# Another order of the same instructions on all five engines of a one-core kernel

## The chip, the core and the metric

The kernel runs on one core of a Trainium2 chip. A core has five engines, each with its own stream of instructions: TensorE (PE in the profile; its weight loads are listed apart as PEld), VectorE (DVE), ScalarE (ACT), GpSimd (POOL) and SyncE (SP, which here only issues DMAs). They wait for one another through semaphores. On-chip memory is SBUF (128 partitions) and PSUM (8 banks of 128 x 512 f32, written by TensorE). The metric is the device time of one execution in microseconds; lower is better.

## What is computed

Two branches of the same input are mixed by a gate. x has 2048 rows of 512, H = 32 heads of 16, Dff = 1376; everything is bf16.

```python
def _A_ref(x, wqkv, w_phi, wo):
    q, k, v = ...                       # x @ wqkv, split into 32 heads of 16
    pq = jnp.einsum("bhsd,hdf->bhsf", q, w_phi)
    pk = jnp.einsum("bhsd,hdf->bhsf", k, w_phi)
    phi_q = concatenate([softmax(pq), softmax(-pq)], axis=-1)
    phi_k = concatenate([softmax(pk), softmax(-pk)], axis=-1)
    kv = jnp.einsum("bhsf,bhsd->bhfd", phi_k, v)
    z  = jnp.einsum("bhsf->bhf", phi_k)
    num = jnp.einsum("bhqf,bhfd->bhqd", phi_q, kv)
    den = jnp.einsum("bhqf,bhf->bhq", phi_q, z)[..., None] + 1e-6
    return (num / den) ... @ wo
def _B_ref(x, w1, w2):
    return relu(x @ w1) @ w2
g = sigmoid((x * gate_w).sum(-1, keepdims=True))
return g * a + (1 - g) * b
```

## The kernel before

The work is written as a graph of 616 named tasks (`_Graph`, line 81). A task is one or a few instructions of one engine, with the tasks that it depends on. Which task follows which on an engine is a list of names for each engine, `ORDER` (line 17). `schedule` checks that each list holds every task once and that no task stands ahead of one that it needs on its own engine; `emit` then issues the instructions in the order of the list, with a semaphore wait in front of a task wherever a task of another engine, or a DMA, has to be done first. An engine does its list strictly in order, so a task that waits holds up all that stand behind it. (`dur` and `lat` of a task are notes that nothing in the kernel reads.)

The names, with m a tile of 128 rows (16 of them), c a chunk of 512 rows (4), k a block of 128 columns of Dff, and J one of 18 jobs (k0 to k8 and q0 to q8; the first seven of each kind take two tiles, the last two one):

- Head: xa0, xa1 load the first chunk of x; xt and xe transpose it through TensorE (L325) and copy it into XT. wkT, wqT, x1, x2, x3 are transposing loads from HBM (L269). f1_j and f0_j (L356) fold w_phi into the key and query weights, fe1 and fe0 (L317, L319) copy the result. v (L374) makes the values, ve (L379) evicts them.
- Branch B: h (L397) is a block of x @ w1, rl (L415) its relu into HT; hr, rr (L405, L421) do the last 96 columns together with the gate's dot product, which gv (L391) puts into w1 as a column; gr (L423) takes the gate out, and ge, gp, go make its two factors. ht (L426) is a DMA transpose of the last block into HT.
- Feature maps, a chain for each job J: pr (TensorE, L454, bank 0 and 1) -> ev (ScalarE, L479) -> mx and mn (VectorE, L483, L485) -> t1 and t2 (GpSimd, L492) -> ex (ScalarE, L497) -> sm and rc (VectorE, L499, L503, L523) -> for a key job nm (GpSimd, L506), for a query job ra and nm (GpSimd, L525, L529).
- Keys: kv (TensorE, L513) adds a tile to kv and z in banks 6 and 7; after kv15, kn and kz (VectorE, L544, L546) take them out.
- Queries: tq (SyncE, L532) is a DMA transpose of a normalised tile, 256 KB, into one of six places of PHQ; nd (TensorE, L556) two halves of num and den; rd and o (VectorE, L562, L564) divide and apply the gate; to (SyncE, L569) is a DMA transpose of the result, into one of four places of OT.
- Output: b (TensorE, L577; L598 for the last tile) is relu(..) @ w2 for a tile, a (L583, L609) adds the attention branch @ wo in the same bank; oe (ScalarE, L628; L616 and L619 for the last tile) scales and evicts; st (ScalarE's queue, L631) stores 128 KB.

PSUM banks are few: h, b and a share banks 3, 4 and 5 in turn. The bank of a block is set by its number in the graph, not by its place in ORDER, so h0_0, h0_3 and h0_6 share bank 3, and a block waits for the eviction (rl, fe, gr, oe) of the block that had the bank before it. In the same way b2 waits for gr3, b7 for oe4 and b8 for oe5. nd has three banks in turn; ev has three places in PB, ex four in FT.

The order is fixed by hand for the first 19 TensorE tasks, warm0 to h0_0, and for the first tasks of ScalarE, VectorE and GpSimd (`follow`, line 100); the DMA loads keep theirs among themselves.

Of the kernel before, what the change touches and what calls it, by code (L numbers as in the profile page):

```python
# [15 lines left out]

ORDER = {
    "sp": (
        "xa0 wva xa1 wvb w1a wphi wkT w1b x1 gw w1c wqT x2 x3 w2a w2b ht1 wo ht0 tq1 tq0 tq2 tq3 to0 to1 ht2 to2 "
        "tq4 tq5 to3 tq6 tq7 to4 to5 ht3 tq8 tq9 to6 to7 tq11 tq10 to8 to9 tq12 tq13 to11 to10 tq14 tq15 to12 "  # L20
        "to13 to14 to15 st15_1 "
    ),
    "pool": (
# [5 lines left out]
    ),  # L29
    "act": (  # L30
# [8 lines left out]
    ),  # L39
    "dve": (  # L40
# [10 lines left out]
    ),  # L51
# [10 lines left out]
    ),  # L62
}

# [615 lines left out]
```

## Time and profile before

| | us |
|---|---|
| median of the 3 runs shown (lowest, highest) | 151.71 (151.42, 151.9) |
| the profiled execution | 151.17 |
| its span, first to last instruction | 149.2 |
| TensorE: busy, share of the span | 144.9, 97% |
| VectorE | 110.8, 74% |
| GpSimd | 109.7, 74% |
| ScalarE | 91.1, 61% |
| granted TensorE clock | 1.00 of full speed |

The profile covers one execution. It lists each engine's busy time; a group "L454 PE MATMUL PS<-WP,XT" is line 454, TensorE, a matmul that reads the tiles WP and XT and writes PS. Times of matmuls overlap one another in the records, and a few per cent of matmul records can be missing, so the weight loads (PEld) show the order and the holes better than the matmuls do. The wait of an engine is given with what ended it ("<- POOL FT L506"). The DMA view gives for each kind of transfer the count and the median time from issue to landing. The profile names no tasks; a row is put to its task by counting the engine's instructions along its ORDER list, since every engine keeps to its list.

### The profile page before, as it was taken

What the parts mean: (1) busy time and instruction counts of PE and PEld (TensorE: products, weight loads), DVE (VectorE), ACT (ScalarE), POOL (GpSimd) and SP (SyncE); (2) the same over time, 40 slices, a digit from 0 to 9 for tenths busy, and PEclk for the clock granted to TensorE, in tenths of its full rate; (3) what the DMA queues carried; (4) which work ended last, traced back from release to release, by engine and by line L of the source; (5) the groups of instructions that cost most, each with busy time, mean ns of one, the idle gap of its engine ahead of it and who ended that gap; (6) DMA issues with size and microseconds to landing.
All of it is one profiled execution on the core that took longest, in us unless ns stands there. A gap on an engine that the chain in (4) does not pass through costs nothing.

```text
span 149.2 us, 2538 instructions
## 1 busy us (share of the span) xinstructions
PE 144.9 (97%) x968; PEld 73.0 (49%) x984; DVE 110.8 (74%) x169; ACT 91.1 (61%) x127; POOL 109.7 (74%) x73
## 2 busy tenths in 40 slices
PE   7899999999999999999999999999999999999994
PEld 2454444454454645444547445444545454544553
DVE  0542679999995499989569899999979987817501
ACT  3347769997886888966896854476535443303131
POOL 4000599999999999999999999999958795060000
PEclk9999999999999999999999999999999999999999
DMA  5999999500003400000000061847495964787423
GB/s 140 295 199 223 259 166 276 191 0 0 4 2 94 116 7 0 0 0 0 4 0 0 0 141 32 151 104 186 102 172 109 245 156 107 135 208 211 106 73 108
DMA packets 45524, 16.11 MB, mean 108 GB/s; under 512 B 39272, under 2 KB 45256, under 8 KB 45512
## 3 DMA queue, kind: packets, MB, share of 16 engines
q1 hardware_dynamic: 43208, 13.89, 42.3%
q10 hardware_dynamic: 2304, 2.06, 4.3%
q8 instruction: 8, 0.13, 0.4%
q14 instruction: 4, 0.03, 0.1%
HBM read 4.41 MB, written 2.10 MB: 44 GB/s over the span
## 4 chain that ended last, share of the span: by engine, by line
PE 94%; DMA 3%; issue 1%; SPq 1%; DVE 0%
PE PS L577 24%; PE PS L397 23%; PE PS L454 19%; PE PS L374 9%; PE PS L583 9%; PE PS L513 3%; DMA FT<-in_A_x_dram 3%; PE PS L556 3%; PE PS L405 2%; PE PS L598 2%; PE PS L356 1%; PE PS L609 1%; SPq L265 1%; PE PS L325 0%; DVE OSB L619 0%
## 5 line engine op out<-in xcount | busy, mean ns | idle before, releaser
L492 POOL TENSOR_TENSOR TS<-PB,MX 128x1024 bf16<-128x1024 bf16 (+1 forms) x18 | 30.8, 1716 | 13.9 <-DVE MX L483 13.9
L499 DVE TENSOR_REDUCE ZB<-FT 128x128 f32<-128x2048 bf16 (+1 forms) x18 | 36.6, 2037 | 4.6 <-ACT FT L497 4.5
L397 PE MATMUL PS<-XT,W 128*128 128x512 bf16 x155 | 37.7, 379 | 0.3
L577 PE MATMUL PS<-W,HT 128*128 128x512 bf16 (+1 forms) x161 | 37.0, 379 | 0.2
L497 ACT ACTIVATE FT<-TS 128x2048 bf16<-128x2048 bf16 (+1 forms) x18 | 31.0, 1720 | 4.5 <-PE PS L513 2.4
L492 POOL TENSOR_TENSOR TS<-MN,PB 128x1024 bf16<-128x1024 bf16 (+1 forms) x18 | 30.8, 1720 | 0.1
L454 PE MATMUL PS<-WP,XT 128*128 128x512 bf16 x126 | 30.1, 379 | 0.1
L506 POOL TENSOR_TENSOR FT<-FT,SC 128x2048 bf16<-128x2048 bf16 (+1 forms) x9 | 29.5, 3285 | 0.0
L415 ACT ACTIVATE HT<-PS 128x512 bf16<-128x512 f32 x40 | 22.8, 601 | 6.3 <-PE PS L397 6.2
L628 ACT ACTIVATE OSB<-PS,OMG 128x512 bf16<-128x512 f32 x15 | 10.2, 685 | 23.5 <-PE PS L583 23.5
L479 ACT ACTIVATE PB<-PS 128x1024 bf16<-128x1024 f32 (+1 forms) x18 | 16.8, 932 | 12.3 <-PE PS L454 8.1
L577 PEld LDWEIGHTS PS<-W,HT 128*128 128x128 bf16 (+1 forms) x165 | 15.5, 97 | 17.4 <-ACT OSB L628 0.3
L397 PEld LDWEIGHTS PS<-XT,W 128*128 128x128 bf16 x160 | 15.0, 98 | 17.5 <-ACT HT L415 1.0
L483 DVE TENSOR_REDUCE MX<-PB 128x64 bf16<-128x1024 bf16 (+1 forms) x18 | 19.5, 1082 | 5.4 <-ACT PB L479 5.4
L485 DVE TENSOR_REDUCE MN<-PB 128x64 bf16<-128x1024 bf16 (+1 forms) x18 | 19.2, 1075 | 0.3 <-ACT PB L479 0.2
L454 PEld LDWEIGHTS PS<-WP,XT 128*128 128x128 bf16 x128 | 12.1, 98 | 14.0 <-DVE WP L319 0.4
L529 POOL TENSOR_TENSOR FT<-FT,SR 128x1024 bf16<-128x1024 bf16 (+1 forms) x9 | 15.6, 1736 | 0.6
L374 PE MATMUL PS<-WV,XT 128*128 128x512 bf16 x61 | 15.5, 379 | 0.2
L583 PE MATMUL PS<-WO,OT 128*128 128x512 bf16 x58 | 14.4, 378 | 0.1
L564 DVE SCALAR_TENSOR_TENSOR OTM<-PS,EG,RD 128x256 bf16<-128x256 f32 x32 | 14.1, 466 | 0.4
L562 DVE RECIPROCAL RD<-PS 128x16 f32<-128x16 f32 x32 | 7.0, 238 | 8.2 <-PE PS L556 7.9
L379 ACT ACTIVATE VS<-PS 128x512 bf16<-128x512 f32 x16 | 9.5, 607 | 3.0 <-PE PS L374 3.0
(54 smaller groups left out, 96.3 us busy)
## 6 DMA issues: line engine op xcount, KB each, us to landing
out_dram<-OSB ACTq DMA_DIRECT2D x15, 128.0 KB, 2.5
W<-in_B_w_dram SPq DMA_DIRECT2D x1, 1280.0 KB, 8.2
W<-in_B_w_dram SPq DMA_DIRECT2D x2, 512.0 KB, 5.0
FT<-in_A_x_dram SPq DMA_DIRECT2D x2, 256.0 KB, 3.4
WV<-in_A_wqkv_dram SPq DMA_DIRECT2D x2, 256.0 KB, 3.7
WO<-in_A_wo_dram SPq DMA_DIRECT2D x1, 512.0 KB, 4.6
W<-in_B_w_dram SPq DMA_DIRECT2D x1, 352.0 KB, 3.6
PHQ<-FT SPq DMA_TRANSPOSE x16, 2.8
```

Source lines behind the costliest of these rows:

```text
L374: last = q.matmul(PS[:, b, :], XT[:, j, m * P:(m + 1) * P], WV[:, j, :], start=(j == 0), stop=(j == ND - 1))
L397: last = q.matmul(PS[:, b, :], W1[:, j, k * P:(k + 1) * P], XT[:, j, chunk(c)], start=(j == 0), stop=(j == ND - 1))
L415: add(f"rl{a}_{k}", "act", lambda q, a=a, k=k, b=b: q.activation(HT[:, k, chunk(a)], PS[:, b, :], ACT.Relu), (f"h{a}_{k}",), dur=0.6)
L454: last = q.matmul(PS[:, n, :], XT[:, j, m * P:(m + 1) * P], WP[:, s, j, :], start=(j == 0), stop=(j == ND - 1))
L483: add(f"mx_{J}", "dve", lambda q, sl=sl, w=w, i=pbg: q.tensor_reduce(MX[:, sl, 0:w * H], i, AX.X, ALU.max), (f"ev_{J}", old("t1")), dur=0. ...
L485: add(f"mn_{J}", "dve", lambda q, sl=sl, w=w, i=pbg: q.tensor_reduce(MN[:, sl, 0:w * H], i, AX.X, ALU.min), (f"ev_{J}", old("t2")), dur=0. ...
L492: add(f"{tn}_{J}", "pool", lambda q, o3=o3, a3=a3, b3=b3: q.tensor_tensor(o3, a3, b3, ALU.subtract), (f"{'mx' if sg == 0 else 'mn'}_{J}", ...
L497: add(f"ex_{J}", "act", lambda q, fs=fs, ts=ts, w=w: q.activation(FT[:, fs, 0:w * F], TS[:, ts, 0:w * F], ACT.Exp), (f"t1_{J}", f"t2_{J}", ...
L499: add(f"sm_{J}", "dve", lambda q, fs=fs, sl=sl, w=w: q.tensor_reduce(ZB[:, sl, 0:2 * w * H], FT[:, fs, 0:w * F].rearrange("p (g d) -> p g ...
L506: add(f"nm_{J}", "pool", lambda q, f3=f3, sl=sl, w=w: q.tensor_tensor(f3, f3, SC[:, sl, 0:2 * w * H].unsqueeze(2).to_broadcast([P, 2 * w * ...
L577: last = q.matmul(PS[:, ab, :], HT[0:r, k, m * P:(m + 1) * P], W2[0:r, k, :], start=(k == 0), stop=False)
L583: last = q.matmul(PS[:, ab, :], OT[:, m % NOT, t, :], WO[:, t, :], start=False, stop=(t == ND - 1))
```

## The change

The five lists of `ORDER` are replaced by others. No other line differs. Each list holds the same tasks; no instruction, size, buffer, bank or dependency is changed.

```diff
--- before.py
+++ after.py
@@ -16,49 +16,49 @@
 
 ORDER = {
     "sp": (
-        "xa0 wva xa1 wvb w1a wphi wkT w1b x1 gw w1c wqT x2 x3 w2a w2b ht1 wo ht0 tq1 tq0 tq2 tq3 to0 to1 ht2 to2 "
-        "tq4 tq5 to3 tq6 tq7 to4 to5 ht3 tq8 tq9 to6 to7 tq11 tq10 to8 to9 tq12 tq13 to11 to10 tq14 tq15 to12 "
+        "xa0 wva xa1 wvb w1a wphi wkT w1b x1 gw w1c wqT x2 x3 w2a w2b ht1 ht0 tq0 ht2 wo tq1 tq2 tq3 to0 to1 to2 "
+        "tq4 tq5 to3 ht3 tq6 to4 tq7 tq9 tq8 to5 to6 to7 tq10 to8 tq11 tq12 to9 tq13 to10 tq14 tq15 to11 to12 "
         "to13 to14 to15 st15_1 "
     ),
     "pool": (
-        "iota_r iota_i iota_c gwz pads ones t1_k0 t2_k0 t1_k1 t2_k1 t1_k2 t2_k2 nm_k0 t1_k3 t2_k3 t2_k4 t1_k5 "
-        "t1_k4 nm_k2 nm_k1 t2_k5 t2_k6 t1_k6 nm_k3 t1_k8 t1_k7 t2_k7 t2_k8 nm_k4 t2_q0 t1_q0 nm_k5 t1_q1 t2_q1 "
-        "nm_k6 t1_q2 ra_q0 t2_q2 nm_q0 nm_k7 nm_k8 ra_q1 nm_q1 t1_q3 t2_q3 t1_q4 ra_q2 nm_q2 t2_q4 t2_q5 ra_q3 "
-        "nm_q3 t1_q5 t1_q6 ra_q4 nm_q4 t2_q6 ra_q5 nm_q5 t1_q8 t2_q7 t1_q7 t2_q8 ra_q6 nm_q6 ra_q7 nm_q7 ra_q8 "
+        "iota_r iota_i iota_c gwz pads ones t1_k0 t2_k0 t1_k1 t2_k1 t2_k2 t1_k2 nm_k0 t2_k3 t1_k3 t1_k4 t2_k4 "
+        "nm_k1 t1_k5 t2_k6 t1_k6 t2_k5 nm_k2 t2_k7 nm_k3 t1_k7 t2_k8 nm_k4 t1_k8 t1_q0 t2_q0 nm_k5 nm_k6 t1_q1 "
+        "t2_q1 ra_q0 t1_q2 nm_q0 t2_q2 nm_k7 nm_k8 ra_q1 nm_q1 t1_q3 t2_q3 t1_q4 ra_q2 nm_q2 t2_q4 ra_q3 nm_q3 "
+        "t1_q5 t2_q5 ra_q4 nm_q4 t2_q6 t1_q6 t1_q7 t2_q7 ra_q5 nm_q5 ra_q6 nm_q6 t2_q8 t1_q8 ra_q7 ra_q8 nm_q7 "
         "nm_q8 "
     ),
     "act": (
-        "xe00 xe10 xe20 xe30 ve1 ve2 ve3 fe1_1 fe1_3 ve0 rl0_0 ev_k0 rl0_3 rl0_1 rl0_2 ev_k1 rl0_6 rl0_4 ev_k2 "
-        "ex_k0 rl0_5 ev_k3 rl0_9 ex_k1 rl0_8 ev_k4 ex_k2 rl1_0 rl0_7 rl1_1 ev_k5 rr0 ve4 ex_k3 ev_k6 rl1_4 rl1_2 "
-        "ve5 rl1_7 rl1_3 ve6 ev_k7 rl1_5 ve7 rr1 rl1_8 ve8 rl1_6 ve9 rl1_9 ge1 ex_k4 ve10 ev_k8 ex_k5 ve11 rl2_1 "
-        "rl2_2 ev_q0 ex_k6 rl2_4 rl2_0 ev_q1 rl2_5 ve12 ge0 ex_k7 rl2_3 ev_q2 gp0 rl2_6 rl2_9 rl2_7 rl2_8 ve13 "
-        "ev_q3 rl3_1 ex_k8 rl3_0 ex_q0 ve14 rl3_3 ev_q4 rl3_4 gp1 rl3_7 rl3_6 rr2 ex_q1 rr3 ge2 ve15 rl3_2 rl3_9 "
-        "ev_q5 rl3_5 ex_q2 rl3_8 ge3 ev_q6 ex_q3 oe0 oe1 ex_q4 st1 ev_q7 oe2 oe3 ex_q5 st3 ev_q8 oe4 oe5 gp2 "
-        "ex_q6 st2 st4 st0 gp3 oe6 ex_q7 oe7 ex_q8 st7 oe8 oe9 st9 st8 oe10 oe11 st5 st6 st10 st11 oe12 oe14 "
-        "oe13 st12 st13 st14 oe15_0 st15_0 "
+        "xe00 xe10 xe20 xe30 ve1 rl0_0 fe1_3 fe1_1 ve3 ve2 rl0_3 ev_k0 rl0_6 rl0_1 ev_k1 rl0_4 rl0_2 ve0 ev_k2 "
+        "ex_k0 rl0_7 rl0_5 ev_k3 ex_k1 rl0_8 ev_k4 ex_k2 rl0_9 rl1_0 ev_k5 ve4 rr0 rl1_1 ve5 ex_k3 rl1_3 ve6 "
+        "ev_k6 rl1_2 ex_k4 rl1_4 ve7 rl1_7 rl1_6 ve8 rr1 rl1_5 rl1_9 ev_k7 ve9 rl1_8 rl2_0 ev_k8 ex_k5 ve10 "
+        "rl2_3 ev_q0 ex_k6 ve11 rl2_2 ev_q1 rl2_6 rl2_1 ve12 rl2_5 rl2_8 ex_k7 rl2_9 rl2_4 ev_q2 ve13 rl2_7 "
+        "rl3_1 ex_k8 ge1 ev_q3 rl3_0 rl3_4 ex_q0 ve14 gp1 rr2 rl3_3 rl3_7 ev_q4 ex_q1 ve15 rr3 rl3_6 ge3 rl3_2 "
+        "ev_q5 gp3 ge2 rl3_5 ge0 rl3_9 ex_q2 rl3_8 gp0 ev_q6 ex_q3 oe0 gp2 oe1 ex_q4 st0 ev_q7 oe2 oe3 ex_q5 oe4 "
+        "st3 ex_q6 ex_q7 oe5 ev_q8 oe6 oe7 ex_q8 oe8 st4 st1 st6 st2 oe9 st9 oe10 st5 oe11 st10 st7 st11 oe12 "
+        "oe13 oe14 st13 st8 st14 st12 oe15_0 st15_0 "
     ),
     "dve": (
-        "ident xe01 xe11 xe21 xe31 shift blk wbd3 wbd2 row4 mk wbd1 wbd0 fe1_0 fe1_2 mx_k0 mn_k0 mx_k1 mn_k1 "
-        "mx_k2 mn_k2 sm_k0 rc_k0 mx_k3 mn_k3 mx_k4 gv mn_k4 sm_k2 mx_k5 gr0 sm_k1 rc_k2 sm_k3 mx_k6 rc_k1 mn_k5 "
-        "mn_k6 mx_k7 rc_k3 fe0_0 gr1 fe0_3 fe0_2 fe0_1 sm_k4 mx_k8 rc_k4 mn_k8 mn_k7 sm_k5 mx_q0 mn_q0 mx_q1 "
-        "sm_k7 mn_q2 mx_q2 rc_k5 mn_q1 sm_k6 rc_k6 sm_q0 mx_q4 sm_k8 rc_q0 mn_q3 rc_k8 rc_k7 gr2 sm_q1 gr3 mn_q4 "
-        "mn_q5 rc_q1 mx_q3 kn0 kz1 kn1 kz0 sm_q2 rd0_0 rd0_1 o0_0 o0_1 rd1_0 rd1_1 o1_0 o1_1 mx_q5 rc_q2 go0 "
-        "rd2_1 rd2_0 o2_1 o2_0 sm_q3 rd3_0 rd3_1 o3_1 o3_0 rc_q3 mx_q6 sm_q4 rd5_0 go1 rd4_0 mn_q6 o5_0 rd4_1 "
-        "o4_0 o4_1 rd5_1 o5_1 rc_q4 sm_q5 rd6_0 mn_q7 o6_0 rd6_1 mx_q8 o6_1 mx_q7 rd7_1 rd7_0 rc_q5 o7_0 o7_1 "
-        "sm_q6 rd8_1 rd8_0 o8_0 go2 o8_1 mn_q8 rd9_0 rc_q6 rd9_1 o9_0 o9_1 rd10_0 o10_0 sm_q7 sm_q8 rd11_0 o11_0 "
-        "rd11_1 o11_1 rd10_1 o10_1 rc_q7 rc_q8 rd12_1 rd12_0 o12_1 o12_0 rd13_0 o13_0 rd14_0 rd13_1 o13_1 o14_0 "
-        "go3 rd14_1 o14_1 rd15_0 rd15_1 o15_1 o15_0 oe15_1 "
+        "ident xe01 xe11 xe21 xe31 shift blk wbd2 row4 mk wbd3 wbd1 wbd0 fe1_0 fe1_2 mx_k0 mn_k0 mx_k1 mn_k1 "
+        "mn_k2 mx_k2 sm_k0 gv rc_k0 mx_k3 mn_k3 mx_k4 sm_k1 mn_k4 gr0 sm_k2 mn_k5 rc_k1 mx_k5 mx_k6 sm_k3 mn_k6 "
+        "rc_k3 rc_k2 gr1 fe0_1 fe0_2 fe0_0 mn_k7 fe0_3 sm_k4 mx_k7 sm_k5 mn_k8 rc_k5 rc_k4 mn_q1 mx_q0 mx_k8 "
+        "mn_q0 sm_k6 mn_q2 mx_q1 rc_k6 sm_k8 mn_q3 mx_q2 rc_k8 sm_q0 rc_q0 mx_q3 gr2 sm_k7 mx_q4 mn_q4 gr3 rc_k7 "
+        "sm_q1 mx_q5 rc_q1 kz0 kn0 kn1 kz1 sm_q2 rd0_0 rd0_1 o0_0 o0_1 rd1_1 rd1_0 o1_1 o1_0 rc_q2 mn_q5 go0 "
+        "rd2_1 rd2_0 o2_1 o2_0 sm_q3 rd3_0 rc_q3 rd3_1 o3_0 o3_1 mx_q6 sm_q4 rd4_0 rd4_1 o4_0 o4_1 rc_q4 rd5_1 "
+        "rd5_0 mn_q6 go1 o5_0 sm_q5 o5_1 rd6_0 rd6_1 o6_0 o6_1 mx_q7 mn_q7 rd7_1 rd7_0 o7_0 rc_q5 o7_1 sm_q6 "
+        "rd8_0 rd8_1 o8_0 o8_1 rc_q6 rd9_0 rd9_1 o9_0 mn_q8 go3 go2 mx_q8 o9_1 sm_q7 rd10_1 rd10_0 o10_1 o10_0 "
+        "sm_q8 rc_q8 rc_q7 rd11_1 rd11_0 o11_0 rd12_0 o11_1 rd12_1 o12_0 o12_1 rd13_0 o13_0 rd14_0 rd13_1 o13_1 "
+        "o14_0 rd14_1 o14_1 rd15_1 o15_1 rd15_0 o15_0 oe15_1 "
     ),
     "pe": (
-        "warm0 xt0a xt0b xt1a xt1b v0a v1a xt2a xt2b xt3a xt3b warm1 v2a v3a v0b v1b v2b v3b h0_0 f1_0 f1_1 f1_2 "
-        "f1_3 h0_1 pr_k0 h0_3 h0_2 pr_k1 h0_6 h0_4 pr_k2 h0_5 h0_7 pr_k3 h0_9 h0_8 pr_k4 h1_1 h1_0 gt pr_k5 v4 "
-        "hr0 h1_3 pr_k6 v5 kv0 h1_4 h1_2 pr_k7 h1_7 v6 h1_5 hr1 v7 h1_8 v8 f0_0 h1_6 v9 h1_9 pr_k8 kv1 f0_3 v10 "
-        "kv2 f0_2 h2_2 kv3 f0_1 v11 kv4 h2_1 h2_0 pr_q0 h2_4 kv5 v12 kv6 kv7 pr_q1 h2_5 h2_3 pr_q2 v13 h2_8 h2_6 "
-        "h2_7 h2_9 pr_q3 h3_1 h3_0 kv8 kv9 kv10 v14 kv11 pr_q4 h3_3 h3_4 v15 h3_6 h3_7 hr2 kv12 kv13 hr3 pr_q5 "
-        "h3_2 h3_9 h3_5 b2 kv14 h3_8 kv15 b1 nd0_1 nd1_0 nd0_0 pr_q6 nd1_1 b0 nd2_1 nd2_0 pr_q7 nd3_0 a0 nd3_1 "
-        "a1 b3 b4 a2 nd5_0 nd4_0 a3 nd4_1 b5 nd5_1 b6 pr_q8 nd6_1 nd6_0 a4 nd7_0 a5 nd7_1 b7 b8 nd8_0 nd9_0 "
-        "nd8_1 a6 a7 nd9_1 b9 nd10_0 b10 a8 nd11_0 nd11_1 nd10_1 a9 b11 b12 nd12_1 nd12_0 a10 a11 nd13_0 nd13_1 "
-        "nd14_0 b13 nd15_0 nd14_1 a12 nd15_1 b14 a13 a14 b15 a15_0 a15_1 "
+        "warm0 xt0a xt0b xt1a xt1b v0a v1a xt2a xt2b xt3a xt3b warm1 v2a v3a v0b v1b v2b v3b h0_0 f1_0 f1_3 f1_2 "
+        "f1_1 h0_3 pr_k0 h0_6 h0_1 pr_k1 h0_4 h0_2 pr_k2 h0_7 h0_5 pr_k3 h0_9 h0_8 gt pr_k4 hr0 h1_0 pr_k5 v4 "
+        "h1_3 h1_1 kv0 v5 pr_k6 v6 h1_2 h1_4 kv1 h1_6 h1_5 pr_k7 v7 h1_7 v8 kv2 hr1 h1_9 v9 f0_1 h1_8 f0_2 pr_k8 "
+        "f0_0 h2_0 v10 f0_3 kv3 h2_3 h2_2 pr_q0 kv4 v11 kv5 pr_q1 h2_6 h2_1 h2_5 v12 pr_q2 h2_9 h2_8 kv6 kv7 "
+        "h2_4 v13 kv8 kv9 h3_0 h2_7 h3_1 pr_q3 hr2 h3_4 kv10 kv11 v14 h3_3 kv12 pr_q4 h3_7 kv13 v15 h3_6 hr3 "
+        "pr_q5 h3_2 b2 h3_5 h3_9 kv14 h3_8 kv15 b1 nd0_0 nd0_1 pr_q6 nd1_1 nd1_0 b0 nd2_0 nd2_1 pr_q7 nd3_0 a0 "
+        "nd3_1 a1 b3 b4 nd4_0 nd4_1 a2 a3 nd5_0 nd5_1 b5 b6 nd6_0 nd6_1 a4 pr_q8 nd7_1 nd7_0 b7 nd8_0 a5 nd8_1 "
+        "nd9_0 a6 b8 nd9_1 b9 a7 a8 nd10_1 nd10_0 b10 nd11_1 b11 nd11_0 a9 nd12_0 a10 nd12_1 nd13_0 b12 nd14_0 "
+        "nd13_1 nd14_1 b13 nd15_1 a11 nd15_0 a12 b14 a13 a14 b15 a15_0 a15_1 "
     ),
 }
 
```

## Prediction

> **What bounds the kernel now.** I read the page's busy times, the chain of waits, a table of busy time by stretch, and then, for the margins, the waits and the time lines of GpSimd, VectorE, SyncE and TensorE. The page and the stretches:
>
> ```profile
> PE 144.9 (97%) x968; PEld 73.0 (49%) x984; DVE 110.8 (74%) x169; ACT 91.1 (61%) x127; POOL 109.7 (74%) x73
> PE 94%; DMA 3%; issue 1%; SPq 1%; DVE 0%
> ...
> 9.20:16.40 7.20, 7.14 (x44) 3.50 (x45) 3.06 (x7) 5.33 (x10) 0.00 (x0) 1.00 0.93 219
> 16.40:89.40 73.00, 72.58 (x497) 36.71 (x503) 62.30 (x59) 58.16 (x83) 72.96 (x36) 1.00 0.26 59
> 89.40:99.90 10.50, 10.39 (x83) 5.47 (x84) 9.85 (x22) 5.44 (x6) 10.34 (x8) 1.00 0.47 90
> 99.90:131.90 32.00, 31.79 (x200) 15.57 (x204) 27.12 (x56) 14.94 (x18) 23.48 (x20) 1.00 0.73 157
> 131.90:147.10 15.20, 15.06 (x112) 8.28 (x110) 5.23 (x18) 3.65 (x6) 1.05 (x1) 1.00 0.53 139
> ```
>
> The columns of the stretches are length, then busy us (instructions) of PE, weight loads, DVE, ACT, POOL, then granted clock, DMA share, GB/s. TensorE is the bound everywhere from 9.2 us: over 9.20 to 147.10 it is busy 136.96 of 137.90, so the page leaves it 0.94 idle. Part of that is not idle at all: 984 weight loads stand against 968 matmul records, and each missing 512-column record shows as a hole of about 0.2. Adding the matmuls at their own pace (0.216 each for 512 columns, 1.73 for eight, by the chain of waits) from 9.2 us gives an end about 0.2 before the real one. So an order can take 0.2 to 0.9 out of this execution and no more. The second thing to see is the column before the clock: from 16.4 to 89.4 GpSimd is busy 72.96 of 73.00. It is a second bound, and the two meet:
>
> ```profile
> PEld PS L513 <- POOL FT L506: 0.2, 1, 0.2
> ```
>
> That is kv15: its weight loads wait for nm_k8 (GpSimd, done 89.36), and its matmuls start at 89.50 with no hole before them. GpSimd has about 0.1 to spare there.
>
> The third limit is the margin of the transposing loads of the last third (SyncE issues, then a landing, then the matmul that uses it):
>
> ```profile
> OT<-OTM SPq DMA_TRANSPOSE x16, 2.4
> ...
> DMA to landing us min/median/max: 2.3/2.4/4.4
> ...
> 94.99 2.58 SPq L569 DMA_TRANSPOSE OT<-OTM  x2
> ...
> 103.00 1.27 SPq L569 DMA_TRANSPOSE OT<-OTM  x1
> ...
> 115.79 2.65 SPq L569 DMA_TRANSPOSE OT<-OTM  x2
> ...
> 121.61 2.97 SPq L569 DMA_TRANSPOSE OT<-OTM  x2
> ```
>
> The second of the pair at 94.99 is to1, issued at 96.31: at 2.4 it lands at 98.7, and a1 loads its weights at 98.97, 0.25 later. In the same way to3 (103.00) lands 0.35 ahead of a3 (105.71). to6 (115.79) took 3.9 and landed 0.1 ahead of a6 (119.82). The second of the pair at 121.61 is to9, issued at 123.39. It is the one with 4.4, and it landed at 127.8, 0.05 ahead of a9 (127.85). None made TensorE wait in this execution; all four have less than 0.4 to spare, while single landings differ by 2.
>
> What makes a landing late can be seen too. In 107.6 to 109.6 us:
>
> ```profile
> q8 instruction: 1, 0.02, 3.1%
> ...
> PHQ<-FT SPq DMA_TRANSPOSE x1, 4.4
> ```
>
> An instruction fetch of 16 KB lies inside the window; tq6 and tq7, in flight or issued around it, took 4.3 and 4.4 where the median of their kind is 2.8. Another lies at 125.6, in to9's flight. And to6 has the stores st2, st4, st0 beside it (3.9). So a late landing costs 1.5 to 2.0.
>
> By the Trainium skill, Runtime: NRT & Kernel Launch, section "Instruction fetch mechanics", crossing a 16 KiB block of instructions is "mostly hidden". For the fetching engine the trace agrees (TensorE shows no hole at 107.7 or 125.6); for transposing loads in flight it differs, by the 1.5 to 2.0 above. By that rule moved fetches would be worth nothing and the sum below would be 151.7.
>
> **The change, part by part.** No instruction is added, removed or resized: TensorE's 984 weight loads and their matmuls, 169 VectorE, 126 ScalarE and 69 GpSimd instructions, and the DMA issues (54 on SyncE, 16 on ScalarE) keep their sizes. Only places move. The sum of TensorE's work stays; what can change is waits.
>
> *The head.* TensorE's order up to h0_0 is the same. f1_3 and f1_1 change places, and ScalarE does rl0_0 ahead of fe1_3, fe1_1. h0_0's result is there at about 10.3, so rl0_0 (0.60) ends at 10.9, where ScalarE began its first fe1 before (10.91). Both fe1 then end near 12.0, together with VectorE's fe1_2 (11.98). pr_k0 starts as before (12.1), GpSimd's t1_k0 too (16.4). Cost 0, bounds 0 to 0.1. The cover is that tie; without it all of GpSimd's stretch moves.
>
> *GpSimd's stretch, 16.4 to 89.4.* Ahead of nm_k8 both orders have the same GpSimd tasks, so nm_k8 can end no earlier, and later by each stall. gv stands ahead of rc_k0 now (VectorE, one more start of about 0.08); nm_k0 followed rc_k0 by 0.1, so 0 to 0.1. The sharp place is nm_k6. Before:
>
> ```profile
> 68.61 3.67 POOL L506 TENSOR_TENSOR FT<-FT,SC 128x2048 bf16<-128x2048 bf16 x1
> ...
> 75.98 3.68 POOL L506 TENSOR_TENSOR FT<-FT,SC 128x2048 bf16<-128x2048 bf16 x1
> ...
> 71.83 0.95 DVE L503 RECIPROCAL SC<-ZB 128x128 f32<-128x128 f32 x1
> ```
>
> nm_k5 runs from 68.61, nm_k6 from 75.98, and rc_k6, which nm_k6 needs, is done at 72.78: 3.2 to spare. In the new order nm_k6 follows nm_k5 at once, at 72.24. VectorE does mn_q2, mx_q1, rc_k6 in this order, and mn_q2 waits for ev_q2, which ScalarE does after rl2_8, ex_k7, rl2_9, rl2_4. TensorE's count puts h2_8 at 64.2; its result is there 1.1 after that, 65.3 to 65.4. From start to start those four take 0.48, 0.95, 0.48, 0.48 (the same kinds before), so ev_q2 starts at 67.8 and takes 1.02: 68.8. mn_q2 68.9, mx_q1 1.12 later, rc_k6 71.1 to 72.05. Margin 0.2, and less if h2_8 is later. The same VectorE run goes on to gr3 (sm_k8 at 72.4, mn_q3, mx_q2, rc_k8, sm_q0 76.5, rc_q0, mx_q3, gr2, sm_k7, mx_q4, mn_q4: 83.85), and b2 needs gr3 for its bank at 84.1; before it was 85.63 for 85.80. Cost here 0 to 0.3; I take 0.1.
>
> *The transposes.* ht2 and ht3 (1.27 of SyncE each) leave their places ahead of to2 and behind to5. ht3 now stands behind to3, where SyncE waits for nm_q3 anyway. ht2 stands behind tq0, whose nm_q0 comes one task sooner, and is issued near 85, with wo behind it (landing about 5 later, first used by a0 at 98). The start of the tail stays: nm_q1 ends at 91.64 at the earliest, then tq2, tq3, to0, to1 as before. to1 keeps its 0.25 ahead of a1, to0 its 0.57. After that the margins grow. to3 goes out at 102.3, not 103.0, and a3 is where it was: 1.0. nm_q4 comes after one t task less of 1.9 and without GpSimd's wait of 1.4 for rc_q4, ending about 109.8, not 113.1. That carries tq8 and tq9, to5 and to6: to6 out at 113.7, landing 116.1, for a6 now at 117.4: 1.3 where it was 0.1. to9 out at 124.1 to 125, landing 126.5 to 127.4, for a9 now at 130.2: 2.8, or 1.3 if the fetch falls on it. to10 out at 126.7, for a10 at 131.2: 2. tq14 has 1.7 ahead of nd14_0. In this execution this gains nothing, since no such wait was paid. In executions where landings are later it gains what was paid for to3, to6 and to9.
>
> *ScalarE's stores.* st1, st2, st4, st6 now go out in one bunch behind oe8, near 126. The nearest rows for a bunch: three stores made to6 1.5 late; four at 135.7 made to12 0.3 late. to10 has 2 to spare, so 0. oe5 now stands behind ex_q7 (t2_q7 done 116.05, so ex_q7 to 117.2, oe5 to 117.8); b8 needs its bank at 118.3: 0.5 to spare, cost 0 to 0.2.
>
> **The sum.** The profiled execution took 151.17: span 149.2 and 1.97 around it. Into it go +0.1 for nm_k6 and gr3, and -0.1 of the few holes: 151.2. The median of the runs shown is 151.71, 0.54 over the profiled one. What those runs lost isn't in a trace. At one end all of it is outside the span (0 to be gained), at the other all is late transposes (0.54). Four margins were under 0.4 and one of the four (to1) is unchanged; I take a little under half as gained: 151.71 + 0.0 - 0.2 = 151.5.
>
> **The rivals.** *GpSimd runs dry at nm_k6* (slower): if ev_q2 or h2_8 is later than counted, each 0.1 beyond the margin of 0.05 to 0.2 goes through nm_k8 to kv15, and TensorE stands, with b1, nd0 and the whole tail behind it. One more ScalarE task of 0.60 ahead of ev_q2 or one VectorE task of 1.1 in the wrong place gives 0.4 to 1.0 less what is now spare: 152.3. Slower by more than the bound from 0.6 late on. For it: two tight places on one run of VectorE. Against: GpSimd had 0.1 to spare before, too, and paid nothing. *The runs' 0.54 is late transposes, and it all goes* (faster): 151.2 less a little, 151.1. For it: margins of 0.05 and 0.1 against landings that vary by 2. Against: to1 keeps 0.25. *The change does nothing to the time*: 0.54 is outside the span and all new margins hold: 151.7.
>
> **How the numbers follow.** Forecast 151.5, a gain too small to tell: 0.31. Nothing changes, 151.7: 0.17. GpSimd dry, 152.3: 0.29. All of the 0.54 gone, 151.1: 0.23. About 0.3% (0.45) is what a measurement of this kernel can tell from no change, so faster means under 151.25 and slower over 152.17. Faster 0.24, same 0.47, slower 0.29. The likeliest case alone spans 151.2 to 151.9. The range for 8 in 10 reaches to 150.9 (all of the 0.54 and the 0.2 of holes) and to 152.6 (GpSimd dry by 1).
>
> **What would show it.** Right: a span of 149.0 to 149.6, matmuls still without holes from 9.2 us, the four to-landings ahead of their matmuls by 1 and more except to1's. Wrong: a weight load of kv15 (L513) or of b2 (L577) that waits over 0.3, a GpSimd wait ahead of nm_k6 (L506 for L503), or a hole at a1 (L583 for a DMA). If the span shrinks by more than 0.9, the reading of TensorE as the bound is wrong.

## The result and the profile after

The changed kernel takes 152.09 us (median of 22 runs, 151.38 to 153.39), the kernel before beside it 151.41 (22 runs, 150.76 to 151.94). The ratio is 1.0052, 95% interval 1.0033 to 1.0072: slower by 0.7 us between the medians, 0.8 by the ratio. The profiled execution took 151.71 with a span of 150.3, against 151.17 and 149.2.

The page of the changed kernel, its busy times and the engines of the chain that ended last, and three of the stretches of before (columns as there):

```profile
PE 144.8 (96%) x967; PEld 73.1 (49%) x984; DVE 110.9 (74%) x169; ACT 91.4 (61%) x127; POOL 109.6 (73%) x73
PE 84%; DMA 8%; ACTq 2%; SPq 2%; issue 1%; DVE 1%; ACT 1%; DVEq 0%
...
16.40:89.40 73.00, 72.53 (x503) 37.08 (x511) 62.64 (x59) 58.96 (x84) 72.89 (x37) 1.00 0.24 54
89.40:99.90 10.50, 10.39 (x80) 5.20 (x79) 10.13 (x21) 5.60 (x8) 10.42 (x7) 1.00 0.62 130
99.90:131.90 32.00, 31.16 (x200) 15.36 (x203) 26.42 (x58) 14.42 (x16) 24.13 (x21) 1.00 0.76 153
```

The work is the same to 0.3 us on every engine. What changed is the chain: TensorE's share falls from 94% to 84%, a DMA's rises from 3% to 8%. (A share of the chain is not the loss; that is read from the stretches and from the wait.) The stretch to 89.4 lost nothing, the one to 99.9 nothing, the one from 99.9 to 131.9 lost 0.6 of TensorE (31.79 before). The waits of the changed kernel name it, and the chain gives the transfer:

```profile
PEld PS L583 <- DMA OT<-OTM: 0.7, 1, 0.7
...
PE PS L583 <- DMA OT<-OTM: 0.6, 1, 0.6
```

```profile
126.11 5.47 DMA OT<-OTM
131.58 0.05 issue
131.63 1.04 PE PS L583 x4
```

This is to10: issued at 126.11, landed 5.47 later (median of its kind 2.4), and a10 stands until then. Before it, TensorE keeps to the places that the sum of its matmuls gives, within 0.1. After it, all is 0.78 later. In the window of that flight, the DMA view and ScalarE's time line show what else was on the DMA engines:

```profile
q8 instruction: 1, 0.02, 1.6%
q14 instruction: 1, 0.01, 0.5%
issues: line engine op xcount, KB each, median us to landing
out_dram<-OSB ACTq DMA_DIRECT2D x2, 128.0 KB, 4.8
PHQ<-FT SPq DMA_TRANSPOSE x2, 3.4
OT<-OTM SPq DMA_TRANSPOSE x1, 5.5
```

```profile
124.79 1.01 ACTq L631 DMA_DIRECT2D out_dram<-OSB  x2
...
125.84 1.19 ACTq L631 DMA_DIRECT2D out_dram<-OSB  x2
...
144.19 3.36 ACTq L631 DMA_DIRECT2D out_dram<-OSB  x4
```

Rows with ACTq are issues by ScalarE: start, length, number. The first two are st4, st1, st6, st2, four stores of 128 KB in 2.2 us, the last two of them issued around to10 and 4.6 and 4.9 us in flight. In the middle of it, at 127.7, a block of TensorE's instructions (q8, 16 KB) was fetched, and a smaller block (q14, 8 KB) at 127.2. (That q8 is TensorE's is read from e6 below: there TensorE alone gets more instructions, and the fetches on q8 move.) The last row is st13, st8, st14, st12 at the end, where oe15_0 had to stand behind 3.36 us of issuing.

### The profile page after: what moved, and what is told of

It reads as the page before. It is cut to its first block, busy times and chain, and to the rows that moved or that the text cites. A ratio compares the mean times of both kernels' runs of the same rounds, so it can differ in the third digit from the quotient of the medians.

```text
span 150.3 us, 2540 instructions
## 1 busy us (share of the span) xinstructions
PE 144.8 (96%) x967; PEld 73.1 (49%) x984; DVE 110.9 (74%) x169; ACT 91.4 (61%) x127; POOL 109.6 (73%) x73
## 4 chain that ended last, share of the span: by engine, by line
PE 84%; DMA 8%; ACTq 2%; SPq 2%; issue 1%; DVE 1%; ACT 1%; DVEq 0%
PE PS L397 22%; PE PS L577 20%; PE PS L454 18%; PE PS L583 8%; PE PS L374 7%; DMA WT<-in_A_wqkv_dram 4%; DMA OT<-OTM 4%; PE PS L513 3%; PE PS L556 2%; ACTq L631 2%; PE PS L405 2%; SPq L265 2%; PE PS L356 1%; ACT OSB L616 0%; DVE OTM L564 0%
## 5 line engine op out<-in xcount | busy, mean ns | idle before, releaser
L562 DVE RECIPROCAL RD<-PS 128x16 f32<-128x16 f32 x32 | 6.5, 229 | 7.7 <-PE PS L556 7.7
```

## Experiments

Each profile can be cut at two marks: f1_0, which waits for the landing of wkT, and a15_0, TensorE's last product but one. That gives three pieces: the head, the long middle, and the rest. The rest is the time of the execution less the other two, so all that lies outside the span is counted in it; the trace doesn't show on which side of the span that lies.

| profile | to f1_0 | f1_0 to a15_0 | a15_0 to the end | time |
|---|---|---|---|---|
| before | 10.25 | 135.66 | 5.26 | 151.17 |
| changed | 9.88 | 136.44 | 5.39 | 151.71 |
| changed, again (e0) | 10.35 | 136.44 | 4.99 | 151.78 |
| e2 | 10.90 | 136.66 | 5.33 | 152.89 |
| e3 | 10.81 | 136.97 | 4.96 | 152.74 |
| e4 | 10.93 | 135.64 | 4.95 | 151.51 |
| e5 | 11.18 | 135.80 | 4.94 | 151.92 |
| e6 | 10.71 | 135.64 | 4.98 | 151.33 |
| e8, e13 (one kernel) | 10.01, 10.85 | 135.72, 135.64 | 4.96, 4.94 | 150.68, 151.44 |
| e9 | 10.69 | 135.64 | 5.20 | 151.54 |
| e10 | 10.43 | 135.73 | 4.86 | 151.01 |
| e11 | 10.40 | 135.72 | 4.94 | 151.06 |
| e12 | 10.51 | 135.80 | 4.91 | 151.23 |

The ratios below are to the kernel before, measured beside each, with 95% intervals (6 runs of e0, e2 and e3, 12 of each other one).

**e2, the order before with the stores of the changed one.** Only ScalarE's list differs from before:

```diff
-ex_q4 st1 ev_q7 oe2 oe3 ex_q5 st3 ev_q8 oe4 oe5 gp2 ex_q6 st2 st4 st0 gp3 oe6 ex_q7 oe7 ex_q8 st7 oe8 oe9 st9 st8 oe10 oe11 st5 st6 st10 st11 oe12 oe14 oe13 st12 st13 st14
+ex_q4 st0 ev_q7 oe2 oe3 ex_q5 ev_q8 oe4 st3 oe5 gp2 ex_q6 gp3 oe6 ex_q7 oe7 ex_q8 oe8 st4 st1 st6 st2 oe9 st9 oe10 st5 oe11 st10 st7 st11 oe12 oe14 oe13 st13 st8 st14 st12
```

> The order before, with only the 15 whole-tile stores of ScalarE's list moved to where the changed order has them (st4 st1 st6 st2 in one bunch behind oe8, st13 st8 st14 st12 behind the last whole eviction). Theory S (the loss comes from where the stores stand): slower by about as much as the change, ratio 1.003 to 1.008, with about four store issues ahead of oe15_0 taking over 2.5 us in ScalarE's queue. Rival F (instruction fetches hit the transposes, wherever the stores are) and rival O (the orders of the other four engines cost it): ratio 0.998 to 1.002.

Measured: 152.89 against 151.54, ratio 1.0111 (1.007 to 1.0152). The stores alone cost at least as much as the whole change, and more than theory S expected; the two intervals just overlap. The sign that theory S gave for the end did not come: the four stores ahead of oe15_0 took 1.85 us to issue, not over 2.5. In its profile, ScalarE's time line, the chain and the waits:

```profile
128.31 1.91 ACTq L631 DMA_DIRECT2D out_dram<-OSB  x4
132.00 0.69 ACT L628 ACTIVATE OSB<-PS,OMG 128x512 bf16<-128x512 f32 x1 [3.01 <-DMA out_dram<-OSB]
```

```profile
128.70 3.22 DMA out_dram<-OSB
```

```profile
PE PS L577 <- ACT OSB L628: 0.9, 1, 0.9
```

The way is another one, though. In the order before, the bunch goes out at 128.3 and st1, the second of it, lands at 131.9. OSB has eight places, so oe9 may not write before st1 has landed. It stands 3.0 us, b12 needs oe9's bank, and TensorE stands 0.9. So a late store can cost directly, too, through the place that it holds.

e2 also shows what stores alone do to a transpose. to6 has no stores beside it there and landed after 2.4 us. In the four other profiles of the order before (before, e9, e11, e12) st2, st4 and st0 go out around it, and it took 3.9 to 4.2.

**e3, the end's stores earlier**, and **e4, the bunch taken apart**, both from the changed order; **e5** is both.

```diff
 (e3)
-oe13 oe14 st13 st8 st14 st12 oe15_0
+oe13 st12 st8 oe14 st13 st14 oe15_0
 (e4)
-oe4 st3 ex_q6 ex_q7 oe5 ev_q8 oe6 oe7 ex_q8 oe8 st4 st1 st6 st2 oe9 st9 oe10 st5 oe11 st10 st7 st11
+oe4 st1 st3 ex_q6 ex_q7 oe5 ev_q8 oe6 oe7 st2 st4 ex_q8 oe8 oe9 st9 oe10 st5 oe11 st10 st6 st7 st11
```

> The changed order, with st12 and st8 moved up behind oe13, so that two stores and not four stand between the last whole eviction and oe15_0. Theory S: the 0.4 to 0.7 us between a15_0 and the end that the changed kernel lost come back, the wait of a10 stays: ratio 1.000 to 1.003. Rivals F and O: 1.004 to 1.007 as the changed order has it.

> The changed order, with the bunch behind oe8 taken apart: st1 behind oe4, st2 and st4 behind oe7, st6 behind st10. Theory S: to10 lands 2.4 to 3.5 us after its issue instead of 5.5 and a10 doesn't wait, the end stays as in the changed order: ratio 1.000 to 1.004. Rival F: a fetch that falls on to10 makes a10 wait 0.4 us or more still, 1.004 to 1.006. Rival O: 1.004 to 1.007.

> The changed order with both moves of stores. Theory S: neither loss, ratio 0.996 to 1.000 (150.8 to 151.4 us), no wait of a10 and no more than 3.4 us from a15_0 to the end. Rival F: 1.002 to 1.004. Rival O: 1.004 to 1.007.

Measured: e3 1.0072 (1.0045 to 1.01; theory S expected 1.000 to 1.003), e4 1.0022 (1.0003 to 1.0042), e5 1.0012 (0.9993 to 1.0032). Without the bunch most of the loss is gone: the middle is 135.64 again in e4 and 135.80 in e5, as before the change, and a10 doesn't wait. The 0.2% that e4 still has over the kernel before shows in no wait of its profile. The stores at the end are not part of it that could be shown: e3 is no faster than the changed kernel, and the changed kernel's second profile (e0) has 4.99 behind a15_0 where the first had 5.39. In e0 the four stores at the end took 2.9 us to issue, and in e4, where they stand in the same places, 2.6 with 4.95 behind a15_0; only the 3.36 of the first profile shows in the last piece. The other four lists (rival O) cost nothing that e5 could tell.

In e4, the landings of OT in the window of to10, and the two stores that remain near it:

```profile
DMA to landing us min/median/max: 4.3/4.3/4.3
```

```profile
124.97 0.85 ACTq L631 DMA_DIRECT2D out_dram<-OSB  x2
```

to10 is still 1.9 late (theory S expected 3.5 at most, not 4.3); two fetches (8 KB at 128.2, TensorE's 16 KB at 128.4) still fall into its flight. It lands 0.4 ahead of a10. The e3 profile shows the same kind of hit at another place, TensorE's chain at a0:

```profile
94.97 4.01 DMA OT<-OTM
98.98 0.14 issue
```

That is to0, with a fetch at 95.9 in its flight, 4.0 and not 2.4; a0 stood 0.5. In the other profiles of this order that fetch came at 91 to 93, and a0 didn't wait.

**e6, the changed order with its fetches moved.** **e8** is e5 with the same edit, **e9** the kernel before with it, **e0** the changed kernel again, all on one chip.

```diff
-add("warm0", "pe", lambda q: pe_warm(q, (D, D, D, D, D, D, P)), (), dur=1.36)
+add("warm0", "pe", lambda q: pe_warm(q, (P,) * 25), (), dur=1.36)
```

> The changed kernel, with the warm-up matmuls at its head cut from six of 512 and one of 128 columns into 25 of 128: the same columns, 36 more TensorE instructions, so that each later block of TensorE's instructions is fetched about 2.5 us sooner (the seventh near 125, not 127.7). Theory S1 (the bunch of four stores alone makes to10 late): to10 still lands over 4.5 us after its issue and a10 waits 0.5 us or more, ratio 1.004 to 1.008. Theory S2 (bunch and fetch together): to10 lands within 4.5 us, no wait of a10, ratio 0.999 to 1.003.

> The changed order with both moves of stores, and the 36 more TensorE instructions at the head. If fetches that fall on transposes still cost what is left of the loss (S2, F): ratio 0.996 to 1.000. If what is left comes from the other lists (O) or is nothing (S1): 1.000 to 1.003.

> The kernel before, with the 36 more TensorE instructions at its head, fetches about 2.5 us sooner. It shows what the cut warm-up costs by itself and whether the order before gains or loses by where the fetches fall: every theory expects 0.998 to 1.002 unless a fetch falls on to1, to3 or to6, which have under 0.4 us to spare: then 1.003 to 1.005 and a wait of a1, a3 or a6.

> The changed kernel once more, on the chip of the three others: every theory expects 1.003 to 1.007, and in the profile a wait of a10 of 0.5 to 0.9 us behind to10.

Measured: e6 1.0014 (0.9996 to 1.0032), e8 0.9978 (0.9958 to 0.9999), e9 1.002 (0.9997 to 1.0043), e0 1.0058 (1.0037 to 1.0078). With the bunch where the change put it and TensorE's seventh block fetched at 123.7, not 127.7, most of the loss is gone: 151.49 against 152.2 for the changed kernel on the same chip. The landing of to10 in e6 and in e0 (in e0 the window holds a second transfer, and to10's is the largest value):

```profile
DMA to landing us min/median/max: 3.9/3.9/3.9
```

```profile
DMA to landing us min/median/max: 3.0/4.1/5.2
```

Put side by side, the profiles of this order give the time from to10's issue to its landing for each case. The small fetch of 8 KB is in all nine flights:

| | TensorE's fetch ahead of the flight | TensorE's fetch in the flight |
|---|---|---|
| stores apart | 2.95, 2.97, 3.00 (e10, e8, e13) | 3.85, 4.29 (e5, e4) |
| stores in a bunch | 3.85 (e6) | 5.19, 5.46, 5.47 (e0, e3, changed) |

Within a column to10 goes out at nearly the same distance from f1_0 (left 116.9 to 117.1, right 116.2 to 116.8), so the bunch alone costs it about 0.9, and about as much or more beside the fetch.

So it takes the bunch and the fetch together (S2), with one reserve from column to column: in e6 to10 goes out right behind the bunch (stores issued 125.6 to 127.7, to10 at 127.7), in the changed kernel within it (124.8 to 127.0, to10 at 126.1), and part of the difference may be that. The bunch, with a small fetch of 8 KB, leaves to10 at 3.9, and in e6, where to10 was issued 0.8 later, it landed just ahead of a10, 0.06 us; the moved fetch fell on to9 instead, which took 5.1 and had 1.5 to spare all the same. In e4 the fetch without the bunch, in e6 the bunch without TensorE's fetch stay inside the margin; with both it is broken, in three profiles of three: a10 stands 0.8 us in the changed kernel and in e3 and 0.5 in e0 (e0's middle lost the other 0.3 at f1 and a1). The order before shows the fetch at work on to9: that took 4.1 to 4.4 where the fetch fell well inside its flight (before, e2, e9), and 3.0 where it came at the end of the flight or behind it (e12, e11).

**The end.** The trace of SyncE's waits shows a thing that the page doesn't. With the changed SyncE list (80 rows of SyncE in the trace) the last wait ends 0.48 behind the one before it and 1.3 to 1.4 lie outside the span; with the list before (79 rows) it is 0.1 to 0.2 and 1.9. In the third piece the changed list is shorter by 0.3 (4.94 to 4.99 for 5.2 to 5.3), but for the first profile of the changed kernel (5.39). e10 is e8, and e12 the kernel before, without the eight waits on stores that the later ones imply (four rows fewer); e11 is the kernel before with two waits more (one row more); e13 repeats e8.

```diff
 (e10, e12)
-            if name.startswith("st"):
+            if name.startswith("st") and int(name[2:].split("_")[0]) >= NOS:
 (e11, ahead of that loop)
+        for name in ("xa0", "xa1"):
+            nc.sync.wait_ge(sems[name], 16)
```

> The changed order with both moves of stores and the 25 short warm-up matmuls, once more, as the version that may beat both: ratio 0.996 to 1.000, no wait of TensorE over 0.2 us from f1 to a15_0, 135.6 to 135.8 us between them.

> The same, and SyncE waits at the end for st8 to st15 alone (each of them can only be issued after the store eight before it has landed), so SyncE has four waits fewer there. In every profile with the changed SyncE list the last of these waits stands 0.48 us behind the one before it, though its store has landed, and 1.4 us lie outside the span, against 0.1 and 1.9 with the list before. Theory E (how many instructions SyncE has sets where a fixed pause at the end falls): with four fewer the 0.48 goes out of the span again and about 1.9 lie outside, the time rises by 0.2 us or stays, ratio 0.997 to 1.002. Rival H (the end doesn't depend on the count): 0.48 and 1.4 stay.

> The kernel before, with two waits more on loads that landed long ago, ahead of SyncE's last waits. Theory E: the last wait now stands 0.48 us behind the one before, 1.4 us lie outside the span, and from a15_0 to the end of the execution it takes 4.95 us and not 5.2: ratio 0.997 to 1.000. Rival H: 0.1 and 1.9 as before, ratio 0.999 to 1.001.

> The kernel before, with SyncE waiting at the end for st8 to st15 alone. Both theories: 0.1 and 1.9 us as before, ratio 0.998 to 1.002; it shows whether the number of waits at the end costs anything by itself.

Measured: e13 1.0002 (0.9984 to 1.002), e10 0.9981 (0.9963 to 0.9999), e11 0.9986 (0.9965 to 1.0006), e12 0.9996 (0.9975 to 1.0017). In the profile of e11 two idle waits more give 80 rows, a gap of 0.48, 1.36 outside the span, and 4.94 behind a15_0 in place of 5.26: the kernel got 0.3 shorter there by having more to do. So the count matters (E), as far as one profile shows; the timed gain can't be told from none. E failed for fewer waits: e10 and e12 (76 and 75 rows) have the gap of 0.17 again, but 1.6 outside the span and 4.86 and 4.91 behind a15_0, no loss. What pauses there stays open.

No version is shown to beat both kernels. e8 and e13 are one kernel and gave 0.9978 and 1.0002; against the kernel before it is a tie or 0.2% better, the changed kernel, at 1.0052 and 1.0058, is behind it by 0.5 to 0.8%.

## Why the prediction was wrong

Forecast 151.5 and "the same", measured 152.09 and slower: the kernel before, measured beside it, had 151.41. By its own steps:

- *TensorE as the bound, and the count of its places: right.* From f1_0 to a15_0 there are 135.64 to 135.80 us in the ten profiles, of both orders, in which no transposing load or store held it up by more than 0.2. An order can lose time here and hardly win any.
- *The head: right in the order, wrong in what it means.* t1_k0 came 6.2 us behind f1_0 in both kernels, as counted (6.4 in e0). But f1_0 itself, that is the landing of wkT, lay between 9.88 and 11.18 in the profiles, with no edit that goes with it. This is where executions of one kernel differ.
- *GpSimd dry at nm_k6: right as a margin, no cost.* The margin was counted as 0.2 or less. In the changed kernel's GpSimd and VectorE time lines nm_k5 and nm_k6 run as one row without a hole, and rc_k6 ends at 71.82, 0.08 ahead of nm_k6:

```profile
68.19 7.39 POOL L506 TENSOR_TENSOR FT<-FT,SC 128x2048 bf16<-128x2048 bf16 x2
...
70.88 0.94 DVE L503 RECIPROCAL SC<-ZB 128x128 f32<-128x128 f32 x1
```

  gr3 ended 0.12 ahead of b2, and kv15 came 79.17 behind f1_0 (79.16 before). The rival that had the right sign had the wrong mechanism. That its 152.3 lies near the measured time is luck, and the range reached past 152.09 only through it.
- *The margins of the transposes: right for most, and the step that failed is in the next one.* to3, to6 and to9 had 0.58, 0.78 and 4.25 to spare (counted: 1.0, 1.3, 2.8), to1 0.35. In two other profiles of this order to1 held a1 up by 0.1 (e0, e5), and in e5 to5 held a5 up by 0.1.
- *"ScalarE's stores ... to10 has 2 to spare, so 0": wrong, and this is the failed step.* It put the bunch at 0.3 to 1.5 by the nearest rows, singly, and a fetch at 1.5 to 2.0, on to9, singly. Each of the two alone was inside the 2 to spare; added, its own rows give up to 3.5. In the run both fell on to10: 3.1 late (5.47 for 2.4), against about 2.3 to spare, and TensorE lost 0.78. The fetch had been counted to stay near 125; it came at 127.7, since the fetches do not keep their distance from f1_0 when the order changes (115.3 before, 117.8 after; with the uncut warm-up 115.0 to 116.2 in the other profiles of the order before, 117.3 to 118.1 in those of the order after).
- *The sum's second term, "a little under half" of 0.54 as late transposes: not borne out at its size.* With 22 runs the median of the kernel before lies 0.24 over the profiled execution and not 0.54. And 0.04 between a landing and the weight load behind it is no margin: to10 in the changed kernel landed at 131.58, and a10, which stood waiting for it, began at 131.62. By this mark the order before did wait for transposes, for to9 in its first profile and for to6 in e9, e11 and e12, but only 0.03 to 0.17 us each time, by the hole ahead of the weight load. That is less than the scatter of the head. e8 against e9 (0.9978 and 1.002, where order and stores differ) would fit a gain there, but e13 doesn't repeat it.
- *Unforeseen:* the 0.3 that the changed SyncE list wins in the third piece.

By the Trainium skill, DMA: Bandwidth & Descriptors, section "Issuing engines are not separate DMA queues", DMAs of ScalarE and SyncE run on the same 16 DMA engines and interleave. The traces agree: SyncE's to10 took 3.9 beside four of ScalarE's stores (e6) and 3.0 without them (e8, e10, e13). By the Trainium skill, Runtime: NRT & Kernel Launch, section "Instruction fetch mechanics", crossing into a new block of instructions is mostly hidden. The traces agree for TensorE, which shows no wait for a fetch; but transposes beside one landed later, and that was worth 0.5 at a0 (e3) and, together with the bunch, 0.78 at a10.

## What to carry to other kernels

Where the bound engine has no holes, look at a new order for the transfers it depends on, and add up everything that can fall into one flight: the margin has to hold the sum of a bunch of stores and an instruction fetch, not the larger of the two. Stores that nobody waits for can still cost, by the transposes that land later beside them (to6, to10) and by the buffer that they hold (e2); spread them over stretches with few transposes. Cut the time of an execution at fixed marks before comparing: here the head scattered by 1.3 us whatever the order, and the middle repeated to 0.2 where no transfer was late.

## What the runs showed of the hardware

- A DMA transpose of 128 x 512 lands after 2.4 us in most cases here. to10 took 3.0 beside a small instruction fetch of 8 KB, 3.9 with a bunch of four stores besides, 3.9 to 4.3 with TensorE's fetch of 16 KB besides, and 5.2 to 5.5 with both.
- The time of TensorE's fetches moves with the order and between executions: the fifth block came 81.7 to 82.0 us behind f1_0 in four of the five profiles of the changed order with the uncut warm-up, and 85.1 in e3.
- Two idle waits more at the end of SyncE's list took 0.6 us from what lies outside the span and put 0.3 into it (e11); the cause is open.
